# u spread by a product, logits turned behind a unit's outputs, rows of six units made before the search, and the first expert's weights asked in two places

## The chip, the cores and the metric

The kernel runs on one core of a Trainium2 chip. The metric is the device time of one launch in microseconds. The two kernels take the same inputs and give the same output. A profile is one profiled execution; its times are counted from the first instruction.

## The reference

An attention block (RWKV5) feeds a mixture of eight experts. Every one of the 3072 tokens goes to one expert, and every expert takes 384: the pair of token and expert with the largest logit is taken first, then the next, as long as the token is free and the expert has room.

```
r, k, v: (4, 8, 768, 48) float32    w, u: (8, 48)
for t in range(768):
    y[:, :, t] = r_t @ (state + (u * k_t) outer v_t)
    state = w * state + k_t outer v_t
x = y.transpose(0, 2, 1, 3).reshape(3072, 384)
logits = x @ w_gate                                  # (384, 8)
for (token, e) in pairs by falling logit:
    if token is free and counts[e] < 384: assigned[token] = e; counts[e] += 1
for e in range(8):
    out[assigned == e] = relu(x[assigned == e] @ w1[e]) @ w2[e]    # w1 (8, 384, 1024), w2 (8, 1024, 384)
```

## The kernel before

**Attention** (class `Mild`) works on 24 units: a unit is 128 steps of one of the four batches, with all eight heads. `run` writes the order of instructions out by hand (under `tc.manual_schedule`), and every engine keeps to it. The heads lie in four pairs. For unit n:

- `load` asks SP for k, r and v (192 KB each), up to five units ahead. `again` (DVE, L340) copies one head's k and r to a second place, so that every pair lies side by side; the fourth transposes of `turn` need it.
- `keys` (GpSimd, here POOL, L420) multiplies k by a table of decay powers `wk`. `own` (POOL, L426 and L427) multiplies r by k and by `u_bc`, which is u repeated on all partitions; `own_sum` (DVE, L432) sums it to `dd`.
- `turn` transposes k and r on TensorE (PE, `kT_ps` L445, `rT_ps` L448) and copies them out. `diagonal` writes eight diagonal blocks of `AT` from `dd` (ACT, L470). `pairs` multiplies (`g_ps`, L480) and puts the products into `AT` under a mask (DVE, L482).
- `outputs` forms `y_ps` (L516) from the state and from `AT`; ACT copies it to `x` (L532). `keep` updates the state (L495 to L503).
- After every fourth unit, `gate` multiplies x by the gate's weights `wgp` (`lg_ps`, L543), ACT copies the sum to `lg`, PE turns it (`lt_ps`, L551), and ACT writes it to `LG`. `lg_ps`, `lt_ps`, `bad_ps` (from `test`, at unit 12), and `most_ps` (from `guess`) take turns in one bank of PSUM, with the tag `few`.

`start` prepares the tables: `wp` from five small loads, its powers, and `Q`, from which the first unit and the tables `WK` and `WR` are made. `wk_table` turns `WK` into `wk`. The later units have the tables; unit 0 uses pieces of Q.

**The search** (class `Assignment`) finds, for the expert that fills first, its 384 tokens: three rounds of counts on DVE and PE, then a place for every token, then `tokens`, whose last line (L1112) writes the token numbers. `between` lets `some_rows` put work between: `rows` turns x back into rows (`x_ps`, L563), ACT copies them to `xr` (L565), and SP stores them to DRAM as `x_rows` (L569).

**The hand-over.** After the search SP asks for the first expert's w1 (L1163) and w2 (L1165), each 1.5 MB; POOL gathers the expert's rows from `x_rows` in three indirect DMAs (`xg`, L1169). Every engine then reads a flag and takes a branch (L1198): if the search did not settle, another attention and a slower search follow, which do not run with these inputs.

**The experts.** For expert n: `turn` transposes the gathered rows (`xT_ps` L1224, ACT copies L1225), `hidden` makes `h_ps` and its relu (L1233, L1234), `result` makes `o_ps` (L1240), ACT copies it (L1242), and POOL scatters it to the output (L1243). The search for expert n + 1 and its loads run beside this. The planner orders this part, not `run`; two sets of weights take turns (`wpools`), and pools opened here lie in memory that the attention's pools have left.

Of the kernel before, what the change touches and what calls it, by code (L numbers as in the profile page):

```python
# [21 lines left out]
T = 128  # L22
PD = 64
# [253 lines left out]
class Mild:  # L277
# [24 lines left out]
    def open(self, ctx):  # L302
        tc, HP, H, D, B = self.tc, self.HP, self.H, self.D, self.B
        const = self.const = ctx.enter_context(tc.tile_pool(name="m_const", bufs=1))
        self.pool = ctx.enter_context(tc.tile_pool(name="m_work", bufs=2))
        self.xpool = ctx.enter_context(tc.tile_pool(name="m_x", bufs=1))
        self.ps = ctx.enter_context(tc.tile_pool(name="m_ps", bufs=1, space=PSUM))
        self.NK, self.NV, self.NS = 5, 6, 5
        self.krs = const.tile([128, self.NK, 2, H + 2, PD], F32, name="krs")
        self.vts = const.tile([128, self.NV, H, PD], F32, name="vts")  # L310
        self.kss = const.tile([128, self.NS, H, PD], F32, name="kss")
        self.states = const.tile([128, B, HP, PD], F32, name="states")
        self.wp = const.tile([128, HP], F32, name="wp")
        self.wc = const.tile([128, HP], F32, name="wc")
        self.ones8 = const.tile([128, 2, HP, 2, 9], F32, name="ones8")
        self.Q = const.tile([128, 2, HP, 9, 8], F32, name="Q")
        self.chunk = const.tile([128, HP], F32, name="chunk")
        self.WK = const.tile([128, HP, T], F32, name="WK")
        self.WR = const.tile([128, HP, T], F32, name="WR")
        self.wk = const.tile([128, H, D], F32, name="wk")  # L320
        self.u_bc = const.tile([128, H, D], F32, name="u_bc")
        self.wgp = const.tile([128, HP, 32], F32, name="wgp")
        self.mask_f = const.tile([128, T], F32, name="mask_f")
        self.mask = const.tile([128, T], U8, name="mask")
        self.bad = const.tile([128, HP], BF16, name="bad")
        self.xts, self.live, self.lgs = {}, {}, {}
# [15 lines left out]
    def start(self):  # L342
# [3 lines left out]
        with nc.allow_non_contiguous_dma(reason="a row to the partitions"):  # L346
            for eng, z, aa, hh in ((nc.sync, 0, slice(0, half), slice(0, HP, 2)),
                                   (nc.scalar, 1, slice(0, half), slice(1, HP, 2)),
                                   (nc.sync, 0, slice(half, HP), slice(HP + 1, H, 2)),
                                   (nc.scalar, 1, slice(half, HP - 1), slice(HP + 2, HP + 3)),  # L350
                                   (nc.scalar, 1, slice(HP - 1, HP), slice(HP, HP + 1))):
                eng.dma_start(self.wp[z * PD:z * PD + D, aa], self.w[hh].rearrange("h d -> d h"))
        for n, what in ((0, "kr"), (1, "kr"), (0, "v"), (2, "kr"), (1, "v"), (3, "kr"), (2, "v"), (4, "kr"), (3, "v")):
# [6 lines left out]
        nc.scalar.dma_start(self.u_bc.rearrange("p h d -> p (h d)"),  # L360
                            self.u.rearrange("h d -> (h d)").partition_broadcast(128))
        for z in range(2):
            nc.scalar.dma_start(self.wgp[z * PD:z * PD + D, :, 0:self.E],
                                self.wg.rearrange("(a z d) e -> z d a e", z=2, d=D)[z])
        nc.scalar.copy(self.bad, self.ident[:, 0:HP])
        warm = self.ps.tile([128, 2, 512], F32, name="warm_ps", tag="y_ps")
        for i in range(16):
            nc.tensor.transpose(warm[:, i % 2, 0:T], self.ident, self.ident)
# [23 lines left out]
        for i in range(2):  # L392
            powers(i)
        nc.vector.reciprocal(AB[:, 1], AB[:, 0])
        by8 = AB[:, :, :, 1, :].rearrange("p x a i -> p (x a) i").unsqueeze(3).to_broadcast([128, 2 * HP, 9, 8])
        by1 = AB[:, :, :, 0, 0:8].rearrange("p x a j -> p (x a) j").unsqueeze(2).to_broadcast([128, 2 * HP, 9, 8])
        nc.vector.tensor_mul(self.Q.rearrange("p x a i j -> p (x a) i j"), by8, by1)
# [3 lines left out]
                       "r": ((slice(0, M + 2), Q[:, 1, :, M + 1::-1]), (slice(M + 2, T), Q[:, 0, :, 1:T - M - 1]))}  # L401

# [36 lines left out]
    def turn(self, n, raw=None):  # L439
        nc, HP, P = self.nc, self.HP, PD + self.D  # L440
        kr = self.krs[:, n % self.NK]
        key = self.kss[:, n % self.NS] if raw is None else kr[:, 0]
        kT_ps = self.ps.tile([128, HP, T], F32, name="kT_ps")
        for a in range(HP):
            nc.tensor.transpose(kT_ps[0:P, a, :], self.pair(key, a), self.ident)  # L445
        rT_ps = self.ps.tile([128, HP, T], F32, name="rT_ps")
        for a in range(HP):
            nc.tensor.transpose(rT_ps[0:P, a, :], self.pair(kr[:, 1], a), self.ident)  # L448
        kT = self.pool.tile([128, HP, T], F32, name="kT")
        rT = self.pool.tile([128, HP, T], F32, name="rT", bufs=3)  # L450
        if raw == "pieces":
            for t, t_ps, x in ((kT, kT_ps, "k"), (rT, rT_ps, "r")):
                for at, q in self.pieces[x]:
                    nc.vector.tensor_mul(t[0:P, :, at], t_ps[0:P, :, at], q[0:P])
        else:
            if raw:
                nc.vector.tensor_mul(kT[0:P], kT_ps[0:P], self.WK[0:P])
            else:
                nc.scalar.copy(kT[0:P], kT_ps[0:P])
            nc.vector.tensor_mul(rT[0:P], rT_ps[0:P], self.WR[0:P])  # L460
        self.live[n].update(kT=kT, rT=rT)
# [74 lines left out]
    def gate(self, c, bs):  # L536
# [9 lines left out]
        if B - 1 not in bs:  # L546
            return
        lg = self.pool.tile([128, T], F32, name="lg", bufs=1)
        nc.scalar.copy(lg, lg_ps)
# [5 lines left out]
    def rows(self, ns, tag):  # L555
# [8 lines left out]
        xr = self.pool.tile([128, 2, H, D], F32, name="xr", bufs=5)  # L564
# [15 lines left out]
    def run(self):  # L580
        N, B, C, walk = self.N, self.B, self.C, self.walk
        self.start()
        self.live = {n: {} for n in range(N)}
        self.own(0)
        self.again(0)
        self.turn(0, "pieces")
        self.tables()
        self.again(1)
        self.own(1)
# [3 lines left out]
        self.turn(1, "tables")  # L593
        self.pairs(0)
        self.own_sum(1)
        self.diagonal(1)
        self.again(2)
        self.own(2)
        self.keys(0)
        chores = walk.constants()  # L600
        for n in range(N):
            self.load(n + 5, "kr")
            self.load(n + 4, "v")
            if n + 3 < N:
                self.again(n + 3)
                if n < 2:
                    self.keys(n + 1)
                self.keys(n + 3)
                self.own(n + 3)
# [4 lines left out]
            if 0 < n <= B:  # L614
                self.keep(n - 1)
            if n + 1 < N:
                self.pairs(n + 1)
            if n >= B and n % B == 0:
                self.gate(n // B - 1, range(B))
            if n == N // 2:  # L620
                for _ in chores:
                    pass
                self.test()
            if n == N - 3:
                walk.guess_most(self.LG.rearrange("p (b c) e -> p b c e", b=B)[:, :, 0:C - 1, :], AX.XYZ)
            if n == N - 2:
                walk.guess(walk.ps.tile([128, 128], F32, name="most_ps", tag="few"), self.ident)
            if n == N - 1:
                self.rows((0,), "kT_ps")
            self.outputs(n)  # L630
# [4 lines left out]
        self.left = [(n, n + 1) for n in range(1, N - 1, 2)] + [(N - 1,)]  # L635
        self.turns = 0
# [480 lines left out]
def rwkv5_eagle_then_base_layer_balanced(  # L1117
# [28 lines left out]
    wpools = [ctx.enter_context(tc.tile_pool(name="weights0", bufs=1))]  # L1146
    gpool = ctx.enter_context(tc.tile_pool(name="f_g", bufs=2))

    def weights(n):
        wpool = wpools[n % 2]  # L1150
# [8 lines left out]
    def load_weights(number, w1=None, w2=None):  # L1159
        e = nc.values_load(number[0:1, 0:1], engines=(mybir.EngineType.SP,), min_val=0, max_val=E - 1,  # L1160
                           skip_runtime_bounds_check_because="E less a number from 1 to E")
        if w1 is not None:
            nc.sync.dma_start(w1, moe_w1[ds(e, 1)].rearrange("o (c p) f -> p (o c) f", p=128))  # L1163
        if w2 is not None:
            nc.sync.dma_start(w2, moe_w2[ds(e, 1)].rearrange("o (c p) d -> p (o c) d", p=128))  # L1165
# [7 lines left out]
    def fetch(n, fmax, tok):  # L1173
        xg = gpool.tile([128, NC, DX], F32, name="xg")
# [7 lines left out]
    xg = gpool.tile([128, NC, DX], F32, name="xg")  # L1182
    w1, w2 = weights(0)
    with ExitStack() as part:
        mild = Mild(tc, r, k, v, w, u, moe_w_gate, x_dram, LG, ident, only, walk)
        mild.open(part)
        with tc.manual_schedule():
            mild.run()
            walk.between = lambda step: mild.some_rows(1 if step == "each" else 2)
            numbers = []  # L1190
            flag = walk.likely(**first, only=only, on_fmax=lambda fmax: numbers.append(number_of(fmax)))
            walk.between = lambda step: None
            mild.some_rows(99)
            load_weights(numbers[0], w1=w1)
            walk.tokens(first["place"], tok)
            gather(xg, tok)
            load_weights(number_of(first["fmax"]), w2=w2)
    with tc.If(walk.found(flag) < 1):  # L1198
# [6 lines left out]
        load_weights(number_of(first["fmax"]), w1, w2)  # L1205
# [5 lines left out]
    wpools.append(ctx.enter_context(tc.tile_pool(name="weights1", bufs=1)))  # L1211
    xpool = ctx.enter_context(tc.tile_pool(name="f_x", bufs=2))
    hpool = ctx.enter_context(tc.tile_pool(name="f_h", bufs=2))
    opool = ctx.enter_context(tc.tile_pool(name="f_o", bufs=3))
# [4 lines left out]
    def turn(xg):  # L1219
        xT = xpool.tile([128, KD, CAP], F32, name="xT")  # L1220
# [26 lines left out]
    xT = turn(ahead[0])  # L1247
    for n in range(E):
# [4 lines left out]
        for c in range(NC):  # L1253
            if c == NC - 1 and n + 1 < E:
                xT = turn(ahead[0])
# [29 lines left out]
```

## Time and profile before

| what | value |
|---|---|
| median of 3 runs | 443.42 us (442.92 to 443.62) |
| the profiled execution's own time | 444.32 us |
| its span, first to last instruction | 442.6 us |
| PE busy | 403.4 us (91%) |
| DVE, ACT, POOL busy | 178.4, 150.6, 133.2 us |
| mean granted PE clock | 0.95 |
| attention (to the last unit's LG) | 0 to 130 us |
| search and token numbers | 130 to 147 us |
| to the first expert matmul | 147 to 163.4 us |
| experts | 163.4 to 442.6 us |

A line of the timeline reads: start in us, duration in us, engine, line, operation, output from inputs, shapes, count; in brackets, how long the engine stood idle before it and what ended the wait. "SPq" is a queue that issues DMAs. A line of the waits reads: engine, its tile and line, what it waited for: us in total, how often, the longest. PEclk is the granted clock of PE in tenths.

### The profile page before, as it was taken

To read this page: it belongs to the slowest core of one execution; us is meant where nothing else is said; L and a number is where in the kernel's file an instruction comes from. 1 tells how busy PE (TensorE), PEld (TensorE's weight loads), DVE (VectorE), ACT (ScalarE), POOL (GpSimd) and SP (SyncE) were. 2 spreads that over 40 slices of the span, in tenths; PEclk is the share of its full clock that TensorE was granted. 3 is DMA by queue.
4 is the path that set the end of the run, shared out by engine and by line. 5 is a ranking of instruction groups with operands and counts; after the bars stand their busy time and mean duration, and the time that the engine had idled before them with its cause. 6 is when DMAs were issued, how large, how long until landed. Compare 5 with 4: busy or idle time off the path is not lost. (4 is left out here: it accounts for less than half of the span.)

```text
span 442.6 us, 7737 instructions
## 1 busy us (share of the span) xinstructions
PE 403.4 (91%) x2913; PEld 267.4 (60%) x2913; DVE 178.4 (40%) x642; ACT 150.6 (34%) x381; POOL 133.2 (30%) x170
## 2 busy tenths in 40 slices
PE   6898999999989149999999999999999999999993
PEld 5687878778768035565565565565556456556551
DVE  6675866556547425405604604703702703000000
ACT  2685878678726111112111211211202202202210
POOL 6976768668300200210120130031031031201001
PEclk9598999999998758999999999999999999999998
DMA  7995757561008930450360270180090096401000
GB/s 138 213 185 112 146 109 149 101 132 37 1 19 282 330 146 0 160 216 18 104 271 19 70 287 36 28 329 36 9 350 36 2 361 222 146 18 37 0 18 36
DMA packets 94003, 54.33 MB, mean 123 GB/s; under 512 B 77184, under 2 KB 88576, under 8 KB 93952
## 3 DMA queue, kind: packets, MB, share of 16 engines
q1 hardware_dynamic: 90080, 44.05, 34.9%
q0 software_dynamic: 3072, 9.44, 5.6%
q10 hardware_dynamic: 800, 0.21, 0.4%
q8 instruction: 26, 0.43, 0.4%
q14 instruction: 25, 0.20, 0.1%
HBM read 44.25 MB, written 9.44 MB: 121 GB/s over the span
## 5 line engine op out<-in xcount | busy, mean ns | idle before, releaser
L1233 PE MATMUL h_ps<-xT,w 128*128 128x384 f32 x384 | 138.1, 507 | 1.3 <-issue 0.5
L1240 PE MATMUL o_ps<-w,hid 128*128 128x384 f32 x384 | 127.5, 486 | 0.0
L1240 PEld LDWEIGHTS o_ps<-w,hid 128*128 128x128 f32 x384 | 71.9, 190 | 47.2
L1233 PEld LDWEIGHTS h_ps<-xT,w 128*128 128x128 f32 x384 | 69.3, 194 | 45.4 <-issue 11.9
L1234 ACT ACTIVATE hid<-h_ps 128x384 f32<-128x384 f32 x64 | 31.4, 491 | 110.6 <-PE h_ps L1233 108.4
L470 ACT ACTIVATE AT<-ident,dd 128x128 f32<-128x128 f32 x192 | 58.6, 390 | 5.8 <-DVE dd L432 5.8
L1169 POOL DMA_INDIRECT xg<-x_rows,tok x21 | 20.2, 963 | 117.8 <-PE h_ps L1233 64.1
L1243 POOL DMA_INDIRECT out_dram<-o_sb,tok x21 | 20.7, 985 | 109.5 <-ACT o_sb L1242 104.4
L1242 ACT COPY o_sb<-o_ps 128x384 f32<-128x384 f32 x24 | 11.5, 479 | 108.3 <-PE o_ps L1240 87.9
L835 DVE TENSOR_TENSOR own<-counts,same 128x64 f32<-128x64 f32 x21 | 4.7, 225 | 101.2 <-PE counts L847 101.2
L482 DVE COPY_PREDICATED AT<-mask,g_ps 128x512 f32<-128x512 uint8 x48 | 32.6, 732 | 13.7 <-PE g_ps L480 12.5
L480 PE MATMUL g_ps<-rT,kT 48*128 48x128 f32 x384 | 29.7, 297 | 0.0
L516 PE MATMUL y_ps<-AT,vts 128*64 128x128 f32 x384 | 27.5, 288 | 0.0
L480 PEld LDWEIGHTS g_ps<-rT,kT 48*128 48x128 f32 x384 | 25.0, 199 | 4.1 <-issue 3.7
L420 POOL TENSOR_TENSOR kss<-krs,wk 128x384 f32<-128x384 f32 x24 | 24.3, 1015 | 5.1 <-DVE krs L340 2.2
L426 POOL TENSOR_TENSOR rk<-krs 128x384 f32<-128x384 f32 x24 | 24.3, 1013 | 3.4 <-DMA wgp<-in_moe_w_gate_dram 3.4
L427 POOL TENSOR_TENSOR rk<-rk,u_bc 128x384 f32<-128x384 f32 x24 | 24.1, 1005 | 1.9
L1224 PE MATMUL xT_ps<-ident,xg 128*128 128x128 f32 x72 | 11.6, 292 | 13.9 <-remote 11.2
L516 PEld LDWEIGHTS y_ps<-AT,vts 128*64 128x64 f32 x384 | 22.0, 144 | 1.3 <-issue 0.7
L460 DVE TENSOR_TENSOR rT<-rT_ps,WR 112x512 f32<-112x512 f32 x23 | 15.9, 691 | 16.3 <-PE rT_ps L448 16.1
L532 ACT COPY x<-y_ps 128x512 f32<-128x512 f32 x24 | 14.1, 586 | 24.5 <-PE y_ps L516 24.5
L1224 PEld LDWEIGHTS xT_ps<-ident,xg 128*128 128x128 f32 x72 | 9.3, 149 | 18.8 <-issue 12.5
(185 smaller groups left out, 393.2 us busy)
## 6 DMA issues: line engine op xcount, KB each, us to landing
w<-in_moe_w_dram SPq DMA_DIRECT2D x16, 1536.0 KB, 11.1
krs<-in_k_dram SPq DMA_DIRECT2D x24, 192.0 KB, 3.6
krs<-in_r_dram SPq DMA_DIRECT2D x24, 192.0 KB, 3.6
vts<-in_v_dram SPq DMA_DIRECT2D x24, 192.0 KB, 2.9
x_rows<-xr SPq DMA_DIRECT2D x24, 192.0 KB, 2.2
xg<-x_rows,tok POOLq DMA_INDIRECT x21, 6.1
out_dram<-o_sb,tok POOLq DMA_INDIRECT x21, 2.6
u_bc<-in_u_dram ACTq DMA_DIRECT2D x1, 192.0 KB
```

The costliest lines, as they stand in the source:

```text
L420: self.nc.gpsimd.tensor_mul(self.kss[:, n % self.NS].rearrange("p (g h) d -> p g h d", g=2)[:, :, :, 0:D], src, self.wk.rearrange("p (g h) ...
L426: nc.gpsimd.tensor_mul(rk, self.krs[:, n % self.NK, 1, 0:H, 0:D], self.krs[:, n % self.NK, 0, 0:H, 0:D])
L427: nc.gpsimd.tensor_mul(rk, rk, self.u_bc)
L470: nc.scalar.mul(AT[:, z, a, :], self.ident, dd[:, h:h + 1])
L480: nc.tensor.matmul(g_ps[:, z, a, :], kT[rows, a, :], rT[rows, a, :], start=True, stop=True)
L482: nc.vector.copy_predicated(out=AT[:, z], mask=self.mask.unsqueeze(1).to_broadcast([128, HP, T]), data=g_ps[:, z])
L516: nc.tensor.matmul(yv[q * PD:(q + 1) * PD, o // 2, o % 2, :], lhsT, rhs, start=(o // 2, q) not in seen, stop=stop, skip_group_check=True)
L1224: nc.tensor.transpose(xT_ps[:, f, :], xg[:, c, ts(f, 128)], ident)
L1233: nc.tensor.matmul(h_ps, w1[:, f, ts(j, 128)], xT[:, f, :], start=(f == 0), stop=(f == KD - 1))
L1234: nc.scalar.activation(hid[:, j, :], h_ps, AF.Relu)
L1240: nc.tensor.matmul(o_ps, hid[:, j, ts(c, 128)], w2[:, j, :], start=(j == 0), stop=(j == KF - 1))
L1243: nc.gpsimd.indirect_dma_start(out=out_rows[n * NC + c], out_offset=bass.IndirectOffsetOnAxis(ap=tok[:, c:c + 1], axis=0), in_=o_sb, in_of ...
```

## The change

- `u` comes as one row (1.5 KB); a product with a row of ones spreads it over the partitions into PSUM, and ACT copies it to `u_bc`. The gate's weights are loaded at unit 1 (`gate_weights`) and not in `start`. One of five loads of `wp` goes to POOL's queue. `Q` is made in halves, one on POOL, one on DVE.
- `idle` writes transposes of the identity that nobody reads: 16 in `start` (as before, under another name), 6 after the first k transposes, 6 after `turn(0)`, 10 before `tokens` and 20 after it.
- `own`, `again` and `keys` stand elsewhere in the order of the first units; `again(n + 3)` stands ahead of `pairs(n + 1)` from unit 1 on, and `keys` and `own` behind it.
- `gate` ends with the copy to `lg`; the transpose and the write to `LG` are in `logits`, called after `outputs`.
- Rows of units 0 to 3 are made at units 22 and 23, those of units 4 and 5 before the search; the search has 18 left instead of 23. `xr` has four buffers instead of five.
- SP is asked for w1 where the search has its number; ACT asks for w2 after the third copy of the first turned rows. In the arm that does not run, only w1 is loaded.
- `xg` and `xT` live in the pools of the weights (`f_turn0`, opened before the attention, and `f_turn1`); the pools opened after the branch have `reuse_waits="tile"`.

```diff
@@ start
-                                   (nc.scalar, 1, slice(HP - 1, HP), slice(HP, HP + 1))):
+                                   (nc.gpsimd, 1, slice(HP - 1, HP), slice(HP, HP + 1))):
...
-        nc.scalar.dma_start(self.u_bc.rearrange("p h d -> p (h d)"),
-                            self.u.rearrange("h d -> (h d)").partition_broadcast(128))
-        for z in range(2):
-            nc.scalar.dma_start(self.wgp[z * PD:z * PD + D, :, 0:self.E],
-                                self.wg.rearrange("(a z d) e -> z d a e", z=2, d=D)[z])
+        nc.scalar.dma_start(self.u_row, self.u.rearrange("h d -> (h d)").unsqueeze(0))
+        nc.vector.memset(self.one_row, 1.0)
         nc.scalar.copy(self.bad, self.ident[:, 0:HP])
-        warm = self.ps.tile([128, 2, 512], F32, name="warm_ps", tag="y_ps")
-        for i in range(16):
-            nc.tensor.transpose(warm[:, i % 2, 0:T], self.ident, self.ident)
+        self.idle(16, "y_ps")
+        u_ps = self.ps.tile([128, 512], F32, name="u_ps", tag="rT_ps")
+        nc.tensor.matmul(u_ps[:, 0:H * D], self.one_row, self.u_row, start=True, stop=True)
+        nc.scalar.copy(self.u_bc.rearrange("p h d -> p (h d)"), u_ps[:, 0:H * D])
...
-        nc.vector.tensor_mul(self.Q.rearrange("p x a i j -> p (x a) i j"), by8, by1)
+        for x, eng in ((0, nc.gpsimd), (1, nc.vector)):
+            eng.tensor_mul(self.Q[:, x], AB[:, x, :, 1, :].unsqueeze(3).to_broadcast([128, HP, 9, 8]),
+                           AB[:, x, :, 0, 0:8].unsqueeze(2).to_broadcast([128, HP, 9, 8]))
@@ new
+    def gate_weights(self):
+        for z in range(2):
+            self.nc.scalar.dma_start(self.wgp[z * PD:z * PD + self.D, :, 0:self.E],
+                                     self.wg.rearrange("(a z d) e -> z d a e", z=2, d=self.D)[z])
+
+    def idle(self, m, tag):
+        ps = self.ps.tile([128, 512], F32, name="unread_ps", tag=tag)
+        for _ in range(m):
+            self.nc.tensor.transpose(ps[:, 0:T], self.ident, self.ident)
@@ turn
+        if raw == "pieces":
+            self.idle(6, "y_ps")
@@ gate
-        if B - 1 not in bs:
-            return
-        lg = self.pool.tile([128, T], F32, name="lg", bufs=1)
-        nc.scalar.copy(lg, lg_ps)
+        if B - 1 in bs:
+            self.lg = lg = self.pool.tile([128, T], F32, name="lg", bufs=1)
+            nc.scalar.copy(lg, lg_ps)
+
+    def logits(self, c):
+        nc, B, lg = self.nc, self.B, self.lg
         lt_ps = self.walk.ps.tile([128, T], F32, name="lt_ps", tag="few")
@@ run
         self.turn(0, "pieces")
+        self.idle(6, "y_ps")
         self.tables()
         self.again(1)
-        self.own(1)
...
         self.turn(1, "tables")
+        self.own(1)
+        self.again(2)
         self.pairs(0)
         self.own_sum(1)
         self.diagonal(1)
-        self.again(2)
+        self.keys(0)
         self.own(2)
-        self.keys(0)
...
+            if n >= N - 2:
+                self.rows((2 * (n - N + 2),), "kT_ps")
+                self.rows((2 * (n - N + 2) + 1,), "rT_ps")
+            self.outputs(n)
+            if full:
+                self.logits(n // B - 1)
...
         self.gate(C - 1, [B - 1])
-        self.left = [(n, n + 1) for n in range(1, N - 1, 2)] + [(N - 1,)]
-        self.turns = 0
+        self.logits(C - 1)
+        self.rows((4, 5), "g_ps")
+        self.left = [(n, n + 1) for n in range(6, N, 2)]
+        self.turns = 1
@@ hand-over
-            numbers = []
-            flag = walk.likely(**first, only=only, on_fmax=lambda fmax: numbers.append(number_of(fmax)))
+            flag = walk.likely(**first, only=only, on_fmax=lambda fmax: load_weights(number_of(fmax), w1=w1))
             walk.between = lambda step: None
             mild.some_rows(99)
-            load_weights(numbers[0], w1=w1)
+            mild.idle(10, "kT_ps")
             walk.tokens(first["place"], tok)
+            mild.idle(20, "kT_ps")
             gather(xg, tok)
-            load_weights(number_of(first["fmax"]), w2=w2)
@@ experts
-    xT = turn(ahead[0])
+    with tc.manual_schedule(engines={nc.scalar.engine}):
+        xT = turn(0, ahead[0])
+        load_weights(number_of(first["fmax"]), w2=w2, by=nc.scalar)
```

## The prediction, made before the result

> **What bounds the kernel now.** I read the page first: the slices of the span and the granted clock.
>
> ```profile
> PE   6898999999989149999999999999999999999993
> ...
> PEclk9598999999998758999999999999999999999998
> ```
>
> Each digit is 11.1 us. The page's costliest groups are the matmuls of the experts, L1233 and L1240: 138.1 + 127.5 us in 768 records. From slice 16 on (about 180 us) the PE row is 9: the expert part is bound by PE, with one small gap per expert, and what is gained ahead of it shortens the whole one for one. The holes are in slices 0 to 3 and 12 to 15. Both rows dip there: PE waits, and its clock is at half. I then read the waits of PE, longest total first:
>
> ```profile
> PE xT_ps L1224 <- remote: 11.2, 1, 11.2
> PE lt_ps L551 <- ACT lg L549: 4.8, 6, 1.7
> PE kT_ps L445 <- DVE krs L340: 4.2, 2, 2.3
> ```
>
> So three places: the hand-over to the experts (11.2 us once), the turned logits (4.8 us in six waits), the start (4.2 us). The timeline shows each. The first group of logits:
>
> ```profile
> 36.03 1.08 PE L543 MATMUL lg_ps<-x,wgp 128*32 128x128 f32 x32
> 38.49 0.24 ACT L549 COPY lg<-lg_ps 128x128 f32<-128x128 f32 x1
> 38.79 0.33 PE L551 MATMUL lt_ps<-ident,lg 128*128 128x128 f32 x1 [1.68 <-ACT lg L549]
> 39.05 0.67 PE L516 MATMUL y_ps<-rT,states 48*64 48x128 f32 x16
> 40.24 1.95 PE L516 MATMUL y_ps<-AT,vts 128*64 128x128 f32 x16
> ```
>
> PE stands 1.68 us between the gate and lt_ps because the copy lg waits on ACT behind eight diagonal products (36.13 to 38.49). The clock then falls: the 16 outputs at 40.24 take 1.95 us, elsewhere 1.06.
>
> The hand-over, from the last token number to the first expert matmul:
>
> ```profile
> 146.79 0.17 DVE L1112 TENSOR_REDUCE tok_first<-mine 128x3 int32<-128x12 f32 x1
> 147.40 0.41 SPq L1163 DMA_DIRECT2D w<-in_moe_w_dram  x1
> 148.33 0.39 SPq L1165 DMA_DIRECT2D w<-in_moe_w_dram  x1
> 149.65 1.17 POOL L1169 DMA_INDIRECT xg<-x_rows,tok_first  x1 [34.15 <-DMA x_rows<-xr]
> 152.38 0.95 POOL L1169 DMA_INDIRECT xg<-x_rows,tok_first  x1 [0.30 <-issue]
> 157.72 1.51 PE L1224 MATMUL xT_ps<-ident,xg 128*128 128x128 f32 x6 [11.17 <-remote]
> 161.38 0.86 ACT L1225 COPY xT<-xT_ps 128x384 f32<-128x384 f32 x2 [16.17 <-SPq L1198]
> 163.43 1.62 PE L1233 MATMUL h_ps<-xT,w 128*128 128x384 f32 x2 [0.45 <-issue]
> ```
>
> The gathers have their tokens at 146.96 but start at 149.65: POOL waits for the x_rows stores, which SP issues at 0.525 us each until 146.6 (15 in 7.88 us). Then 3 MB of w1 and w2 are in flight with them: the gathers take 7.3 us to land, where the quickest of the kernel takes 1.9. PE's transposes wait for POOL's step after the third landing (157.2). ACT starts its copies only at 161.38: in the built program this copy waits for every DMA lane of SP, so for w2 itself, whose landing SP's own wait ends at 161.2.
>
> **What the Trainium skill says.** "TensorE: Matmul & The Clock Gate", Part 1 (the HAM clock gate): the clock halves after about 3.4 us without enough work and comes back after about 3.4 us of it. The trace agrees: PE's last work is at 146.55 and the clock is 0.50 from 149.63. The same page, Part 4, says transposes do not bring the full clock; the trace disagrees: sixteen row transposes took 3.13 us at 132.67 and 1.70 us at 136.89, with almost only transposes between. So I count filler transposes as work. [...]PE's branch at 147.2 took 3.83 us. "DMA: Bandwidth & Descriptors", Anatomy of one DMA, puts a DMA from GpSimd at about 2.0 us fixed; no direct one is in this trace.
>
> **The change, part by part** (times are of the trace before; minus is gain).
>
> *Start.* The broadcast of u (192 KB) and the two loads of wgp leave the DMA queues, busy at 0.9 to 1.2 from 3 us; r of unit 0, issued at 2.37, landed at 7.75 between them. The row of u, a product of 384 columns and one ACT copy (about 0.46 us, as the wk copy) replace them. One wp load goes from ACT to POOL ahead of ident: POOL's later work slips by 0 to 1.2 us (the longest POOL issue seen is 1.17), and wp, complete at 4.38 now, comes between 0.5 earlier and 0.5 later. Halving Q frees DVE by 0.38 us; POOL pays some 0.8 (288 elements at 1.0 us per 384). Fillers (16, 6, 6 transposes at 0.11 to 0.23 us) stand ahead of kT_ps(0), rT_ps(0) and wk: 0 to 1.5 us of delay, but the clock should then hold where g_ps took 2.08 instead of 1.16 and y_ps 1.97 instead of 1.06. again(2) now goes ahead of the masked copy of unit 0, so the 2.3 us wait of kT_ps goes. On POOL, keys(0) goes ahead of own(2), and waits for wk (about 13.4): rk(2) ends near 16.6 instead of 14.15, so dd(2) comes near 17.1, still inside AT(1)'s work on ACT. Then ACT is next: AT(1) and AT(2) end at 20.2 as before; from there x(0) 0.59, the two wgp issues 0.76 (moved here; kT's copy queues behind them), and three times kT 0.59, AT 2.45, x 0.59 give 20.2 + 1.35 + 10.9 = 32.45 for x(3), on which the first gate waits; it starts at 36.03 now. That is -3.5 if ACT never waits; fillers and POOL work against it. I take **-3.0**, bounds -4.5 and +0.5.
>
> *Logits behind the outputs.* From the gate's start to the outputs' is 3.02 us at unit 4 and 2.02 at 8, 16, 20; without the wait about 1.0. The moved transpose still costs 0.11. So -1.9 and three times -0.9. At unit 12 the product bad_ps shares the bank of lg_ps and itself waits for the lg copy: only -0.3. The clock at unit 4 (5.80 us from one outputs to the next, against 4.19) gives -1.6. LG's copy now queues behind x on ACT, which has room (3.6 busy of 4.19). Sum **-6.5**, bounds -5 and -7.
>
> *Rows ahead.* Units 0 to 3 cost PE four times 0.48 us before the outputs of units 22 and 23, one of them paid today; 0.2 us fills the wait at 125.62: **+1.2**. Units 4 and 5 lie in PE's gap from 129.8 to 131.4. Three pairs leave the end: PE, ACT and six store issues; the last store leaves SP near 143.1 instead of 146.6. The filled gap may keep the clock, and the second count, ready at 134.83, need not wait until 135.47; xr with four buffers instead of five may make ACT wait up to 0.4. **-0.5**, bounds -1 and +0.5.
>
> *w1 early, w2 late.* w1 still stands behind the stores on SP: it leaves near 144 instead of 147.4, and its 1.5 MB, at the 376 to 417 GB/s that the stretches from 150 to 157 show, land near 150.5 with two gathers between. The gathers go at 147.1 instead of 149.65; the third, issued near 150, needs 1.9 to 3 us: 152.5. POOL's step after it: 153. PE's twenty fillers (2.1 to 4.2 us) and its branch (3.83) make PE ready between 152.6 and 154.7; I take 153.5. xT no longer lies in freed memory and waits for no lane: 0.8 us to the first copy, 2.05 from it to the matmuls as now (161.38 to 163.43) give 156.3 against 163.43: **-7.1**, bounds -9 and -4. w2 leaves ACT after the third copy, with a register load ahead of the first relu; PE can run two banks, 4 us, before it needs that relu. With 12.5 us, the slowest landing now, w2 is there by 169.5; the first o_ps comes 17.8 us after the first h_ps, at 174. PE runs cold until 169 now, 5.6 us at half; after, the warm-up runs from the transposes on without the hole: **-1.0**, bounds -2 and 0. Pools by tile and turn change no order in the experts but two matmuls: 0; PE's own 9s cover it.
>
> Sum: -3.0 - 6.5 + 1.2 - 0.5 - 7.1 - 1.0 = -16.9. The profiled execution took 444.32 us for a span of 442.6; so 427.4, and the median of the runs, 443.42, is 0.9 lower: **426.5**.
>
> **Rivals.** (B) The start gives nothing: fillers and POOL's order take what the queues give. For it: POOL is busy almost without a break from 7.85 to 24.46, with the same work to do. Against it: PE's 2.3 us wait is removed by order alone. 429.5. (C) The hand-over stays gated: PE's branch after twenty fillers, or DVE's leave (5.7 us behind its own branch) sets it, and only 3 us are won. Against it: the congestion that stretched those branches is half. 430.6; with B, 433.5. (D) Slower: w2, asked by ACT, comes late. Landing later than 174 stops PE one for one, and the loss passes the gain from about 191 on, 34 us after ACT asked; the slowest landing seen is 12.5. At 195: 448. (E) The change does not do what it says, w1 leaving no earlier because SP's stores still last to 146: the price is in C.
>
> **Chances.** Main 0.60, B 0.15, C 0.17, both 0.03, D 0.03, none of it 0.02. Range 420 to 434: all good bounds together (-1.5, -0.5, -0.5, -1.9, -1.0 against the values taken) give 421.1, the lower end; the upper takes in B and C together. 0.2% is what a measurement of this kernel tells from no change. Faster 0.95, same 0.02, slower 0.03.
>
> **What would show it.** Right: the lt_ps waits gone but for the last, and the clock row without its dip at 40 us; the first gate near 33; gathers issued right behind the token numbers; ACT's xT copies within 1 us of the transposes; the first h_ps near 147.5 (156.3 - 3.0 - 6.5 + 1.2 - 0.5). Wrong: PE's idle before xT_ps still about 10 us, o_ps waiting for w2, or a clock at half past the first gate.

## The result and the profile after

The changed kernel takes 442.53 us (median of 20 runs, 440.72 to 445.6) against 443.18 us (20 runs, 441.77 to 444.96): a ratio of 0.998 (95%: 0.9966 to 0.9999). Predicted were 426.5 us and a range from 420 to 434. Of the 16.9 us that the prediction added up, less than 1 us arrived. The profiled execution took 441.4 us for a span of 439.5, 3.1 us less than the one of before: the two profiles lie further apart than the medians, and a row of the table below is good to a microsecond or two.

The same two rows as before, from the page of the changed kernel (a digit is 11.0 us):

```profile
PE   7688999899998769999999999999999999999993
...
PEclk9959999999999869999999999999999999999999
```

The hole at slices 13 to 15 has become shallow: that is the hand-over, which gained. But the clock has a new dip to half at slice 2 (22 to 33 us), where it was full before; the one of before, at slice 1, is gone. The dip at 40 us, behind the first logits, is gone as predicted. Landmarks from the two timelines, in us:

| | before | after | difference | predicted |
|---|---|---|---|---|
| first gate (4 units done) | 36.03 | 43.10 | +7.1 | -3.0 |
| first to fifth gate (16 units) | 78.26 | 76.37 | -1.9 | -5.6 |
| fifth to last gate | 12.95 | 12.98 | 0.0 | +0.3 |
| last gate to first token numbers | 19.55 | 18.82 | -0.7 | -0.5 |
| token numbers to first h_ps | 16.64 | 10.06 | -6.6 | -7.1 |
| first h_ps to first o_ps | 20.80 | 20.07 | -0.7 | -1.0 |

(Of the logits' -6.5, unit 20's -0.9 falls behind the fifth gate, beside the rows' +1.2.) Everything behind the last gate came close to the size that was worked out. The units lost what they should have gained. The waits of the changed kernel (engine, its tile and line, what it waited for: us in total, times, longest) name who was late:

```profile
DVE dd L442 <- POOL rk L437: 23.6, 15, 3.2
...
POOL kss L430 <- DVE krs L342: 20.6, 17, 3.2
...
PE kT_ps L455 <- POOL kss L430: 8.1, 5, 4.3
```

The second line is the new one: 17 waits of GpSimd's kss for a copy of VectorE that takes 0.20 us. Before, they were 5 waits with 2.2 us. PE's waits for lt_ps fell from 4.8 us to 0.6 as predicted; these took their place, 6.3 of the 8.1 us ahead of the first gate. One turn of the loop, on VectorE and GpSimd alone, from the timeline of the changed kernel (start, duration, engine, line):

```profile
67.83 0.55 DVE L442 TENSOR_REDUCE dd<-rk 128x8 f32<-128x384 f32 x1 [1.60 <-POOL rk L437]
...
68.31 0.68 DVE L472 TENSOR_TENSOR rT<-rT_ps,WR 112x512 f32<-112x512 f32 x1
...
68.90 0.20 DVE L342 COPY krs<-krs 128x96 f32<-128x96 f32 x1
...
69.18 1.01 POOL L430 TENSOR_TENSOR kss<-krs,wk 128x384 f32<-128x384 f32 x1 [0.83 <-DVE krs L342]
...
70.16 1.00 POOL L436 TENSOR_TENSOR rk<-krs 128x384 f32<-128x384 f32 x1
...
71.24 1.01 POOL L437 TENSOR_TENSOR rk<-rk,u_bc 128x384 f32<-128x384 f32 x1
...
72.28 0.55 DVE L442 TENSOR_REDUCE dd<-rk 128x8 f32<-128x384 f32 x1 [1.64 <-POOL rk L437]
```

Read the starts: copy 68.90, kss 0.28 later, first rk 0.98, second rk 1.08, dd 1.04, rT 0.47, and the next copy (73.35) 0.60 later. The sum is 4.45 us, and each step starts when the one before has ended: a closed cycle. dd follows dd at 4.43 to 4.49 us in 12 of the 23 steps.

PE needs 4.19 us for a unit, but 17.91 us for four units with their gate, which is 4.48 for one. So the bare cycle is as long as PE's own work and leaves no room beside it. Where nothing else stands in it, it costs almost nothing: from the second to the third gate and from the fourth to the fifth (18.02 and 17.91 us) the profile shows no wait of PE at all. It costs where other work of VectorE or GpSimd stands in it. From the first to the second gate (20.33 us) they make constants for the search, and dd follows dd at up to 6.02 us; between the third and the fourth (20.11 us) stands the test of unit 12:

```profile
48.62 0.15 DVE L793 TENSOR_SCALAR own_i<-own_i 128x1 int32<-128x1 int32 x1 [2.27 <-POOL own_i L791]
...
51.75 0.65 PE L455 MATMUL kT_ps<-ident,kss 128*112 128x128 f32 x4 [0.81 <-POOL kss L430]
...
84.56 0.18 PE L589 MATMUL bad_ps<-bad,ones 128*128 128x4 bf16 x1 [2.03 <-DVE bad L587]
```

In the first line VectorE waits for a constant that GpSimd makes behind its products; dd stands behind it (49.34), and at its next keys PE waits.

In the kernel before, the copy stood ahead of dd, at the head of an iteration. The dd that needs a copy's products comes in the next iteration, behind that iteration's copy; so the way leads back to a copy only after two units, and the same steps have twice the time.

At the start of the loop the same order costs more. The lines around unit 3's keys:

```profile
20.60 1.32 DVE L494 COPY_PREDICATED AT<-mask,g_ps 128x512 f32<-128x512 uint8 x2
...
21.82 0.19 DVE L342 COPY krs<-krs 128x96 f32<-128x96 f32 x1
...
22.09 1.01 POOL L430 TENSOR_TENSOR kss<-krs,wk 128x384 f32<-128x384 f32 x1 [3.19 <-DVE krs L342]
...
23.15 1.10 PE L455 MATMUL kT_ps<-ident,kss 128*112 128x128 f32 x4 [4.32 <-POOL kss L430]
...
26.07 2.08 PE L492 MATMUL g_ps<-rT,kT 48*128 48x128 f32 x16
...
28.08 1.97 PE L528 MATMUL y_ps<-AT,vts 128*64 128x128 f32 x16
```

In the first iteration again(3) stands even behind the masked copies (20.60), so GpSimd waits 3.19 us and PE 4.32 us. PE's clock halves (21.8 to 32.0 us), and g_ps and y_ps take 2.08 and 1.97 us where they take 1.16 and 1.09 at the full clock.

The hand-over of the changed kernel, the lines that answer to those of before:

```profile
149.09 0.41 SPq L1190 DMA_DIRECT2D w<-in_moe_w_dram  x1
...
151.27 0.17 DVE L1138 TENSOR_REDUCE tok_first<-mine 128x3 int32<-128x12 f32 x1
...
151.73 1.07 POOL L1196 DMA_INDIRECT xg<-x_rows,tok_first  x1 [28.50 <-DVE tok_first L1138]
...
158.37 2.39 PE L1249 MATMUL xT_ps<-ident,xg 128*128 128x128 f32 x9 [3.53 <-DVE last L920]
...
159.33 1.07 ACT L1250 COPY xT<-xT_ps 128x384 f32<-128x384 f32 x2 [12.27 <-PE xT_ps L1249]
...
161.31 0.42 ACTq L1192 DMA_DIRECT2D w<-in_moe_w_dram  x1
```

The first gather starts 0.29 us behind the token numbers (2.69 before), ACT's copies 0.96 us behind the first transposes (3.66 before), and w2 leaves behind the copies. No o_ps waits for w2.

### The profile page after: what moved, and what is told of

Same layout as the page of the kernel before. It is cut to its first block, busy times and chain, and to the rows that moved or that the text cites. A ratio compares the mean times of both kernels' runs of the same rounds, so it can differ in the third digit from the quotient of the medians.

```text
span 439.5 us, 7828 instructions
## 1 busy us (share of the span) xinstructions
PE 406.2 (92%) x2957; PEld 270.9 (62%) x2957; DVE 181.2 (41%) x643; ACT 151.1 (34%) x383; POOL 134.5 (31%) x172
## 5 line engine op out<-in xcount | busy, mean ns | idle before, releaser
L430 POOL TENSOR_TENSOR kss<-krs,wk 128x384 f32<-128x384 f32 x24 | 24.3, 1014 | 30.0 <-DVE krs L342 20.6
L492 PE MATMUL g_ps<-rT,kT 48*128 48x128 f32 x384 | 28.8, 291 | 0.7 <-DVE AT L494 0.7
L528 PE MATMUL y_ps<-AT,vts 128*64 128x128 f32 x384 | 26.6, 282 | 0.0
L442 DVE TENSOR_REDUCE dd<-rk 128x8 f32<-128x384 f32 x24 | 13.2, 550 | 23.6 <-POOL rk L437 23.6
L455 PE MATMUL kT_ps<-ident,kss 128*112 128x128 f32 x84 | 14.3, 296 | 8.1 <-POOL kss L430 8.1
```

What stands on the lines that cost most here:

```text
L430: self.nc.gpsimd.tensor_mul(self.kss[:, n % self.NS].rearrange("p (g h) d -> p g h d", g=2)[:, :, :, 0:D], src, self.wk.rearrange("p (g h) ...
L492: nc.tensor.matmul(g_ps[:, z, a, :], kT[rows, a, :], rT[rows, a, :], start=True, stop=True)
L528: nc.tensor.matmul(yv[q * PD:(q + 1) * PD, o // 2, o % 2, :], lhsT, rhs, start=(o // 2, q) not in seen, stop=stop, skip_group_check=True)
```

## The experiments

Theory O: the place of `again` (and perhaps of `keys` and `own`) makes the cycle and the start's wait. Rival S: the new work of start() delays the units, and the cycle only shows it. Each run stood beside runs of the kernel before on its chip, whose medians were 442.67 to 443.33 us; ratios are to these.

**The unit loop's order put back in the changed kernel** (e1_loop_order).

```diff
+            if n + 3 < N:
+                self.again(n + 3)
+                if n < 2:
+                    self.keys(n + 1)
+                self.keys(n + 3)
+                self.own(n + 3)
             if n + 2 < N:
                 self.own_sum(n + 2)
...
-            if 0 < n < N - 3:
-                self.again(n + 3)
...
-            if n == 0:
-                self.again(n + 3)
-            if n + 3 < N:
-                self.keys(n + 3)
-                self.own(n + 3)
-                if n < 2:
-                    self.keys(n + 1)
```

> The changed kernel with one thing put back: in the unit loop the copy again(n+3), keys(n+3) and own(n+3) stand at the head of an iteration, as before, and not behind the states' update and the pairs. Theory O (the order of the unit loop cost the gain: again behind the turned rT and GpSimd's three products behind again make a loop of 4.45 us that PE's 4.19 us must follow, and at the first unit again(3) behind the masked copy left PE without keys for 4.3 us and its clock low for 11): first gate from 43.1 to 36-37 us, gates 1 to 5 from 76.4 to about 72 us apart, the waits of POOL kss for DVE's again from 20.6 us to under 6; time about 431 us (428 to 434). Rival S (the start's own new work, that is fillers ahead of the turned rows, the product for u, the later keys' weights, delays the units, and the loop only shows it): first gate stays above 41 and the time between 439 and 443. Rival N (PE is bound elsewhere, for instance by ACT's diagonals): waits move from POOL to ACT and the time falls by under 3 us.

Measured: 432.3 us, ratio 0.976 (0.9718 to 0.9803): 10.2 us below the changed kernel. First gate 36.91, first to fifth gate 72.97 us (18.4, 17.9, 18.8 and 17.9 from gate to gate). From its waits:

```profile
POOL states L513 <- DVE states L512: 10.6, 11, 2.4
...
POOL kss L430 <- DVE krs L342: 2.1, 4, 1.0
```

The 20.6 us are 2.1 us. GpSimd's longest wait in the loop is now its states' product, which waits for VectorE's sum; PE, between the first and the fifth gate, waits 0.9 us in all. Rival N falls too: the gain was 10 us, and no wait of PE moved to ACT's diagonals.

**start() put back, the new loop order kept** (e2_start_old): u by its DMA, w_gate's weights at the start, wp on ACT, Q in one piece, no fillers ahead of kT and rT.

```diff
-                                   (nc.gpsimd, 1, slice(HP - 1, HP), slice(HP, HP + 1))):
+                                   (nc.scalar, 1, slice(HP - 1, HP), slice(HP, HP + 1))):
...
-        nc.scalar.dma_start(self.u_row, self.u.rearrange("h d -> (h d)").unsqueeze(0))
+        nc.scalar.dma_start(self.u_bc.rearrange("p h d -> p (h d)"),
+                            self.u.rearrange("h d -> (h d)").partition_broadcast(128))
...
-            self.idle(6, "y_ps")
```

> The changed kernel with start() as before: u spread by the DMA to 128 partitions, w_gate's weights at the start, the last of wp on ACT, Q in one piece on DVE, no fillers behind the first kT and the first rT; the loop order, the logits and the hand-over stay changed. Theory O: the turned r of unit 0 is ready about 2 us sooner, but the units still follow the loop of 4.45 us and the wait for again(3) stays; first gate 41 to 43 us, time 440 to 443. Rival S: the start's work was the cost; first gate 36 to 38 and time about 436.

Measured: 440.66 us (20 runs), ratio 0.9934 (0.9918 to 0.995), first gate 42.72. So S as the main cause falls: the cycle and the late keys stay. But the start is no gain either; it costs some 2 us (the intervals of this run and of the changed kernel do not meet).

**The new loop order alone, in the kernel before** (e3_before_loop_new): the edit of the first experiment, the other way round.

```diff
             if 0 < n <= B:
                 self.keep(n - 1)
+            if 0 < n < N - 3:
+                self.again(n + 3)
             if n + 1 < N:
                 self.pairs(n + 1)
+            if n == 0:
+                self.again(n + 3)
+            if n + 3 < N:
+                self.keys(n + 3)
+                self.own(n + 3)
```

> The kernel before with one part of the change alone: again, keys and own of unit n+3 stand where the changed kernel has them. Theory O: the same two losses appear without anything else of the change: first gate from 36.0 to 41-43 us and some of PE's 0.9 us stalls at the logits hidden by the longer loop; time 448 to 453 us. Rival S: 443 to 445 us, first gate within 1 us of 36.

Measured: 450.13, 452.06 and 454.97 us (a fourth run, at 459.04, stands apart and is not counted), ratio 1.022 (1.017 to 1.0275). The order alone costs the old kernel 9 to 10 us by these few, widely spread runs, and 6 by the profiled executions (450.13 against 444.32). dd follows dd at 4.43 to 4.49 us in 9 steps. The first gate, at 39.49, came earlier than expected; the rest is lost later, from gate to gate (80.8 us against 78.3).

**The last part alone, in the kernel before** (e4_last_part): rows of six units ahead, w1 with its number, the fillers around the tokens, w2 on ACT, pools by turns. Seen from the changed kernel:

```diff
-        for x, eng in ((0, nc.gpsimd), (1, nc.vector)):
...
                 self.gate(n // B - 1, range(B))
+                self.logits(n // B - 1)
...
-            if full:
-                self.logits(n // B - 1)
```

with start(), the order ahead of the loop and the order in it as before.

> The kernel before with the last part of the change alone: rows of six units ahead of the search, w1 asked with its number, fillers around the tokens, w2 behind the turned rows on ACT, pools by turns; start, loop order and logits right behind their gate are as before. By the prediction's steps (rows +1.2, search -0.5, hand-over -7.1, clock -1.0): 436 us (434 to 438), tokens to first h_ps from 16.5 to about 9.5 us. A rival, that the hand-over came out short only because the search began late in the changed kernel: tokens to h_ps above 12 us and 439 us or more.

Measured: 437.08 us, ratio 0.986 (0.983 to 0.9888). Token numbers to first h_ps 10.55 us. The expected 436 us and 9.5 us were 1 us too good; the rival (12 us and more) falls. Its first gate is at 34.42 us, that of the kernel before at 36.03, with the same start and order: so far can one profiled gate be off.

**Only the copy put back** (e9_again_alone): one instruction per unit, in the changed kernel.

```diff
+            if n + 3 < N:
+                self.again(n + 3)
             if n == 1:
                 self.gate_weights()
...
-            if 0 < n < N - 3:
-                self.again(n + 3)
...
-            if n == 0:
-                self.again(n + 3)
```

> The changed kernel with one instruction per unit put back: only again(n+3), VectorE's copy of 0.20 us, stands at the head of the iteration; keys and own stay behind the pairs, which is the same order on GpSimd from the second unit on. Theory O1 (the copy's place alone closes the loop again 0.28, kss 0.98, rk 1.08, rk 1.04, dd 0.47, rT 0.60, sum 4.45 us): all of the loop order's effect returns, units at 4.19 us, 432 us (430.5 to 434) like the version with all three put back. Rival O2 (the place of keys and own behind the pairs matters as much): 436 us or more, with GpSimd's kss still waiting over 10 us for something.

Measured: 432.99 us, ratio 0.977 (0.9742 to 0.9794), as with all three put back. The place of a 0.20 us copy on VectorE is worth 9.5 us; that of keys and own, nothing that shows.

**The copy kept where the change has it, but made a unit further ahead** (f3_copy_a_unit_ahead).

```diff
-            if 0 < n < N - 3:
-                self.again(n + 3)
+            if 0 < n < N - 4:
+                self.again(n + 4)
...
             if n == 0:
-                self.again(n + 3)
+                self.again(3)
+                self.again(4)
```

> The changed kernel with start and order as it has them; the copy stays at its place behind rT and the states, but is made for unit n+4 instead of n+3, so that the loop of VectorE and GpSimd spans two units. Theory O (a cycle that closes once in a unit): the waits of kss for the copy fall from 20.6 us to those of unit 0, dd steps of 4.19 us return, gates 1 to 5 from 76.4 to 73 us, and only the start's late again(3) stays (first gate 40 to 43): 436 to 439 us. Rival P (the copy's place behind rT delays what is behind it on VectorE, whatever unit it is for): 441 to 443 us, dd steps stay at 4.45.

Measured: 436.78 us, ratio 0.987 (0.9851 to 0.9887). Its waits hold one line for this copy, unit 3's:

```profile
POOL kss L430 <- DVE krs L342: 3.2, 1, 3.2
```

First to fifth gate 72.5 us (17.9, 17.9, 18.8 and 17.9 from gate to gate), and the first gate at 41.32. So the two losses come apart: the cycle costs about 5.7 us (442.5 to 436.8; in the profiles 3.9 between the gates and 1.8 ahead of them), the late keys of unit 3 with the low clock behind them about 4 (436.8 to 432.3 to 433.0). Rival P falls: same place on VectorE, no wait.

**All orders and start() put back** (e6_all_orders_start_old): what remains of the change is the logits' place and the last part. Beside the edits of the first two experiments, ahead of the loop:

```diff
         self.again(1)
+        self.own(1)
         self.own_sum(0)
...
-        self.own(1)
-        self.again(2)
         self.pairs(0)
...
+        self.again(2)
+        self.own(2)
         self.keys(0)
-        self.own(2)
```

> The changed kernel with the loop order, the order ahead of the loop and start() all as before: what stays of the change is logits behind outputs and the last part. From the run of the last part alone (437.1 us) and the logits' gain between gates 1 and 5 read in the run with the old loop order (72.97 against 79.05 us): 437.1 - 6.1 = 431.0 us. If the new start is the 2 us loss that the run with the old start showed under the slow loop, this beats the version with the new start (432.3) by 1 to 2.5 us; if that loss was made by the slow loop, the two agree within 0.7 us.

Measured: 430.83 us, ratio 0.973 (0.9701 to 0.9757). Against the run of the last part alone the only difference is where the logits are turned: 437.08 - 430.83 = 6.25 us.

**Loop order and start() put back, the new order ahead of the loop kept** (e7_loop_order_start_old): the edits of the first two experiments together.

```diff
-            if 0 < n < N - 3:
-                self.again(n + 3)
...
-        self.idle(6, "y_ps")
```

> The changed kernel with loop order and start() as before, and the new order ahead of the loop (own(1) behind the turned rows of unit 1, again(2) ahead of the pairs of unit 0, keys(0) ahead of own(2)). Against the version with that order put back as well it tells the worth of this order alone. If the new start is a loss of 2 us in itself: 430 us (429 to 431.5). If the order ahead of the loop gains by itself, this is the faster of the two by 0.5 us or more and its first gate is earlier than 34.4 us.

Measured: 430.57 us, ratio 0.972 (0.9692 to 0.9747). The order ahead of the loop is worth nothing that shows: its first gate is at 35.36, that of the version without it at 35.21.

**The old loop order, without the fillers behind the first kT and the first rT** (e8_loop_no_fillers).

```diff
-        if raw == "pieces":
-            self.idle(6, "y_ps")
...
         self.turn(0, "pieces")
-        self.idle(6, "y_ps")
```

> The changed kernel with the old loop order and without the twice six transposes that nothing reads, behind the first kT and behind the first rT. If the fillers delay the turned r of unit 0 (they took 1.49 us at the low clock between kT and rT): first rT 1.5 us sooner, first gate about 36 us instead of 36.9, 431.3 us. If they keep the clock up as the change has it: the clock of the first 20 us falls, the first g_ps takes 2.08 instead of 1.16 us, and the time is 432.3 or up to 2 us more.

Measured: 431.58 us, ratio 0.974 (0.9716 to 0.9772); first rT at 9.08 instead of 9.70 us, first gate 36.43 instead of 36.91, first g_ps 1.16 us as with them. The fillers brought nothing that shows; that they cost half a microsecond is not shown, since the two intervals overlap.

**In that version, wp's fifth load asked by ACT again** (f4_wp_on_act).

```diff
-                                   (nc.gpsimd, 1, slice(HP - 1, HP), slice(HP, HP + 1))):
+                                   (nc.scalar, 1, slice(HP - 1, HP), slice(HP, HP + 1))):
```

> The version with the old loop order and no fillers around the first kT and rT, and the fifth load of wp asked by ACT again, not by GpSimd ahead of ident. Theory L (GpSimd's memsets, 0.7 us later, run while VectorE wants to read wp, and VectorE's first product stands until they end: 1.7 us instead of 0.17): that product takes 0.17 us again, the powers and Q are ready 1 us sooner, first gate from 36.4 to about 35.4 us, 430.6 us. Rival W (wp itself is complete later through GpSimd's queue): the product starts later or earlier but its 1.7 us stay. Rival U (the product for u and its copy hold unit 0): first gate stays at 36.4 and the time at 431.6 although the product is short.

Measured: 430.52 us, ratio 0.971 (0.9697 to 0.9724), first gate 34.84. The timelines, first with wp's load on GpSimd:

```profile
3.82 1.70 DVE L390 TENSOR_SCALAR ones<-wp 128x4 f32<-128x4 f32 x1 [1.00 <-DMA wp<-in_w_dram]
...
4.54 0.95 POOL L375 MEMSET states<- 128x1024 f32 x1
```

and with it on ACT:

```profile
3.24 0.96 POOL L375 MEMSET states<- 128x1024 f32 x1
...
4.41 0.17 DVE L390 TENSOR_SCALAR ones<-wp 128x4 f32<-128x4 f32 x1 [1.59 <-DMA wp<-in_w_dram]
```

GpSimd's issue of that load waits until VectorE has cleared wp and then takes 0.73 us; both together push GpSimd's memsets by 1.30 us under VectorE's first product of wp, which then stands until they end: 1.70 us instead of 0.17. Theory L holds: the two intervals of the times overlap a little, but the product and the first gate moved as it says. The Trainium skill, "SBUF — State Buffer", section "SBUF: two separate sides", states that VectorE in its two-port modes and GpSimd share one pair of ports as an exclusive lock for a whole instruction. This pair of runs agrees, as VectorE's product ends with GpSimd's memsets; that it is in a two-port mode no trace shows. With this and the fillers undone, the product for u, the later w_gate and the halved Q remain, and the time is that of the old start (430.57): together they gain nothing and cost nothing.

**w2 asked by SyncE behind the gathers** (f1_w2_with_w1), in the version with loop order and start() as before.

```diff
             gather(xg, tok)
+            load_weights(number_of(first["fmax"]), w2=w2)
...
         xT = turn(0, ahead[0])
-        load_weights(number_of(first["fmax"]), w2=w2, by=nc.scalar)
```

> The version with loop order and start() as before, and one more thing put back: w2 is asked by SyncE right behind the gathers, not by ACT behind the turned rows. If w2's [...]transfer beside the gathers delays them (as the prediction's hand-over step has it): gathers land in about 7 us instead of 5, first h_ps 1.5 to 2 us later behind the tokens, 432.3 us (431.5 to 433). If the early w1 and the gathers' place did all of it: 430.6 us as without this edit, and o_ps no earlier.

SyncE asks for w2 at 140.39 us here, 0.26 us behind the start of the first gather. Measured: 432.32 us, ratio 0.977 (0.9753 to 0.9796). Token numbers to first h_ps 12.03 us instead of 10.05: the transposes start 0.9 us later, and behind them the first h_ps waits for a step of SyncE:

```profile
151.71 1.62 PE L1253 MATMUL h_ps<-xT,w 128*128 128x384 f32 x2 [1.40 <-SPq L1219]
```

Of the hand-over's gain, about 1.8 us is w2's place.

**No fillers around the token numbers** (f2_no_fillers_tokens), in the same version.

```diff
-            mild.idle(10, "kT_ps")
...
-            mild.idle(20, "kT_ps")
```

> The version with loop order and start() as before, without the 10 and 20 transposes around the tokens that nothing reads. By the prediction's clock term (-1.0 us for a clock that stays up over the hand-over) the time rises to 431.6 us (431 to 432.5) and the clock in the first 12 us of h_ps falls. If the clock of h_ps is set by the wait itself: 430.6 us, no difference.

Measured: 430.71 us, ratio 0.972 (0.9702 to 0.9744). No difference. In the profiled executions PE's clock in the first 12 us of h_ps was 0.76 without and 0.86 with them, but also 0.76 in the version with all orders put back, which has them.

## Why the prediction was wrong

The parts as the runs priced them, from the kernel before upward; medians of separate measurements, so good to about 1 us each:

| part | predicted | measured | from |
|---|---|---|---|
| rows, search, hand-over, clock behind it | -7.4 | -6.3 | before, last part alone |
| logits behind the outputs | -6.5 | -6.3 | with and without, all else equal |
| start and the order ahead of the loop | -3.0 | +1.5 | all orders and start old, loop order old |
| place of again, keys, own in the loop | not priced | +10.2 | loop order old, changed kernel |
| sum | -16.9 | -0.9 | |

**The step that failed** is a term that the sum does not have: the new place of again(n+3), keys and own inside the loop, taken as free without a reason. The prediction followed again(2) and keys(0) ahead of the loop and passed over these. It took for granted that after the first gate PE sets the pace at 4.19 us and everything else has room ("ACT, which has room (3.6 busy of 4.19)"). The runs show +10.2 us in its place, 9.5 of them by the 0.20 us copy alone: unit 3's copy behind a masked copy, for which PE stands 4.3 us and loses its clock (about 4), and a cycle of 4.45 us over two engines, in which other work on its way is paid (about 5.7). Room on each engine alone is no proof: GpSimd has 3.5 us of work in a unit and VectorE some 3.1, but the new place of the copy puts most of the two in series. The durations were all in the trace of before: the copy 0.20, three products of 1.0, dd 0.55, rT 0.68 make 4.43 us, over 4.19.

**Start.** Predicted -3.0 (bounds -4.5 and +0.5), measured +1.5. "if ACT never waits" was the condition, and ACT waited 3.23 us for the first dd in the changed kernel. That POOL "slips by 0 to 1.2 us" was in the text, but not what it meets: VectorE's first product of wp, which then stood 1.5 us. The load itself came as soon: 2.4 us to landing from GpSimd, 2.3 from ACT before. The transfers of u and w_gate that leave the queues, and what replaces them, were together worth nothing. Rival B, that fillers and GpSimd take what the queues give, came nearest for this step. Of again(2), which now goes ahead of the masked copy, the prediction said that PE's 2.3 us wait goes. The trace of before has two waits for such copies, and it took the wrong one:

```profile
8.06 0.32 PE L445 MATMUL kT_ps<-ident,krs 128*112 128x128 f32 x1 [2.30 <-DVE krs L340]
...
16.19 0.46 PE L445 MATMUL kT_ps<-ident,krs 128*112 128x128 f32 x1 [1.90 <-DVE krs L340]
```

The 2.30 us are unit 0's, whose copy follows the landing of r at 7.75 us; again(2) is the 1.90 us. Neither is left in the changed kernel, where PE is at the product for u until 8.0 us. But again(3), moved behind the next masked copy by the same change, made a wait of 4.3 us.

**Logits.** Right in mechanism and size: -6.3 against -6.5. In the changed kernel most of it can't be seen: from the first to the fifth gate 1.9 us in all are left, because the cycle took the rest.

**Rows ahead.** +1.2 predicted. The run of the last part alone shows 13.88 us from the fifth to the last gate against 12.95: +0.9.

**Hand-over.** First h_ps 10.06 us behind the token numbers; the predicted 156.3 on the axis of before means 9.5. The gathers' start, ACT's copies and w2 did what was worked out, and the gain was twice the 3 us of rivals C and E; D did not occur. That the sum fits is luck in part. The fillers were added ahead of PE's branch (2.1 to 4.2 and 3.83 us); in the trace they run beside it, and the branch takes 5.57 us (151.75 to 157.32). A gather was given 1.9 to 3 us to land; the quickest on record in the trace of before takes 3.0, and here the first takes 6.0 and the third 5.0. The transposes do not wait for the third, as the prediction has it: they start at 158.37, and it lands at 159.3. What is last now is their start, 7.0 to 7.9 us behind the token numbers in every version with w2 behind the copies. The waits put it down to VectorE or to a remote event; but wherever a trace has the first gather's landing, they start 0.2 to 0.9 us behind it, and with the last part of the change PE's branch ends 0.2 to 1.4 us ahead of it. So the landing is the likelier limit; no run moved it alone.

**Clock behind it.** -1.0 predicted, -0.7 in the pair of profiles, but the run without fillers gives no difference in time, and profiled executions of near versions spread from 19.8 to 21.2 us between first h_ps and first o_ps. They follow the moment at which PE's clock is full again: 3.3 us behind the first h_ps in the shortest of these, 6.1 in the longest, 3.8 in the changed kernel and 6.3 before (5.6 in the prediction). Without the 30 fillers it was 5.7, and as much in one version that has them. The size may be right; that the fillers do it is not shown.

**Slower rival.** The one that was given, late w2, was not near. The cycle would have been the better one: it turned a gain of 10 to 12 us into less than 1.

## What to carry to other kernels

When a change moves an instruction in an engine's order, follow it around: who makes its input, who waits for its output, and whether the way returns to the same engine within one iteration. If it does, the sum of that way is a bound of its own, whatever room each engine has, and where it comes near the slowest engine's time, other work that stands on it is paid; giving the loop a second unit of distance, or moving the short instruction ahead, opens it. And before a load goes to GpSimd's queue to spare another one, look what VectorE does at the time when GpSimd's later work will run.

## What was not expected of the hardware

- A VectorE product of 128x4 elements took 1.70 us, and a 128x96 copy 1.01 us (0.20 elsewhere), each beside GpSimd's work: 1.5 and 0.8 us of standing that the profile counts as VectorE's busy time, not as a wait. The first went when GpSimd's work was moved; the copy's was not tested. The product `bad` of unit 12, for which PE waits 2.03 us in the changed kernel, took 0.92 us there and 0.15 with the old loop order.
- The product that spreads u, 2 matmul records of one row by 384 columns, took 1.65 us in the changed kernel and 0.91 and 1.24 in two others; the prediction gave it no time.
- A few microseconds of idle PE cost twice: the 4.32 us for unit 3's keys were followed by some 9 us (to 32.0) of matmuls at half the clock.
